# Retention attention and channel mixer on one core: batch 1's q loaded row per partition and turned by whole products, with a redone order

## The chip, the cores and the metric

One core of a Trainium2 chip runs the whole program in one launch. The metric is the device time of that launch in microseconds (us). Three runs of the kernel before gave 185.78, 186.19 and 189.02 us; their median is 186.19 us.

## The reference

```python
def _attn_ref(q, k, v):                    # q, k, v: (4, 8, 768, 64)
    gamma = 1.0 - 2.0 ** (-5.0 - np.arange(H))
    scale = 1.0 / np.sqrt(D)
    for t in range(S):
        state = gamma * state + np.einsum('bhd,bhe->bhde', k[:, :, t], v[:, :, t])
        y[:, :, t] = scale * np.einsum('bhd,bhde->bhe', q[:, :, t], state)
    ...
def _moe_ref(x, w_tok1, w_tok2, w_ch1, w_ch2):   # x: (4, 768, 512), the heads side by side
    h = np.maximum(x.transpose(0, 2, 1) @ w_tok1, 0.0) @ w_tok2
    u = x + h.transpose(0, 2, 1)
    h2 = np.maximum(u @ w_ch1, 0.0) @ w_ch2
    return u + h2
```

A decaying sum over time (one decay per head) gives y. The mixer then multiplies across time (768 to 256 to 768), adds, multiplies across channels (512 to 1536 to 512), and adds again. All inputs are float32; the kernel computes in float16 with float32 sums.

## The kernel before

**Tiling.** There are four batches of eight heads, and the heads go in pairs, so that a pair fills 128 columns (2 heads of 64). The 768 steps are cut into 6 chunks of 128. `front(b, p)` does the attention of pair p of batch b and the mixing over time; `back(b)` does the mixing over channels of a whole batch. The recurrence is computed by chunks: inside a chunk as masked scores (`L642`, then `L653` with the mask, then `L673`), between chunks through a 64x64 state per head (`L591` sums it per chunk, `L603` carries it on, `L621` and `L623` round it, `L699` applies it).

**The back.** For batch 0, `L829` does the first channel product directly. For the others `widen7` (`L898`) and for all of them `narrow7` (`L1051` and `L1061`) compute it with seven block products in place of eight. The sums and differences of weights that these need are made once, on VectorE: `L1156` (`wsum`) and `L1169`. Evacuations from PSUM are split over ScalarE and VectorE (`L845`, `L909`, `L918`, `L1068` and others).

**How q and k get their layout.** The scores need q and k with the head dimension on the partitions and time along the row. k arrives with one time step per partition (`L495`, 96 rows of packets in the planner's unit, float32 to float16 on the way), is multiplied by its decay in SBUF, one instruction per head (`decayed`, `L533` on ScalarE or `L535` on VectorE), and is turned in one of two ways given by the table `TURNS`, whose three letters are for k, q and u: "t" means six whole 128x128 products with the identity (`L561`) and one copy out of PSUM (`L574`); "x" means a transposing DMA from the SP queue (`L549`). q has a third way, "w": it arrives with six successive time steps per partition (`L492`, long rows), is turned unscaled by twelve half-array products, 64 columns each (`L559`), and is multiplied on the way out of PSUM by a table of decays that depends on time, `gq` in the tile `late` (`L569`, on VectorE). The tile `late` is later used again for the weight sums of `L1169`. Batches 0 and 1 have q in way "w", batches 2 and 3 in way "x".

**The order.** Nothing is scheduled at run time. Each piece of work is an `Op` with its ways (an engine and a cost). The string `ORDERED` gives the order of all ops, two characters per op (a number in base 62 in the order in which the program makes the ops), and `WAYS` has one digit per op that selects its engine where there are two. Filtered by engine, `ORDERED` is the queue of that engine, and each engine works through its queue in that order: PE (the matmuls), ACT, DVE, POOL (the loads, through one software DMA queue) and SP (stores and transposing DMAs). `arrange` (lines 111 to 253) walks through these queues with a table of costs to choose banks and buffers. Where PE has nothing to do in the first 21 us of that plan, products with zeros are put in (`L1196`).

**Loads.** POOL's queue starts with batch 0's q, k and v, then `wt` (the time weights, first and second part), then batch 1's, mixed with the channel weights `wc` (first `wc1`, whose four parts are a0 to a3, then `wc2`, parts b0 to b2), then batches 2 and 3.

Of the kernel before, what the change touches and what calls it, by code (L numbers as in the profile page):

```python
# [110 lines left out]
def arrange(ops, BANKS, seq, ways):  # L111
# [144 lines left out]

DIGITS = "0123456789abcdefghijklmnopqrstuvwxyzABCDEFGHIJKLMNOPQRSTUVWXYZ"
ORDERED = (
    "0e0c070d01080f05000h0306090g0i1h1i1l0m0a1j0j1k0b1m1V0n1W1v1w0k1R1x1S1y1A1T0l1z1n1U1B1o0o2r2s25261p2t1q0p292u"
    "1r2v2a1s1C0q311t322w0r1u3528331D361E1F0t1X1Y27342G1Z2K0s1G2F202x21222J2b232y2I240x1H2H2d2z2c1I0u2e2A2L2f2B2C"  # L260
    "3f2g1J0w2D3h1M1K2h2E3i1N0v372i1L2N2M382O2P392j0y1O3a2m3b2Q3g3c4L3j3d2R0D3k3e2k3l3m2S3n0A3o2n2T3p2l1P3q2W0z2U"
    "1Q3r2X2V2p0B4M3s2Z2o3t2Y3w0C303u5k3B4d3x3C3F2q490H3z4a3v3D3A4b4ead4cag3GaeaN0EaO3Eb23yaPavaf5lb30Faw3Paxah3Q"
    "aQ0Gaias3Tb4aR3SaZaSb03R0N4nb13H4p4f3Iap4qay3Jaq3Kaj4rar0Iaz4g3L3Vat3MaA4o3UaKau0R3NaLaB4h4iakaC3Oam4j4Han4k"
    "3WaE1dao3X0JaFalaH3Y02aIaD1fbhaMbk3ZaT1eaGaUaJ400MaV1gbb41be4Ibnbibc4lbp4204bo4Jbdbl430O4Kbfbm4519bjbr440Kb8"
    "461ab54mb6bsb9bg0Q1baWbaaX474s1cbPb70LaY4u4NbQ4VbJ4Obw4P4Xby4Ybx4Q4t5h5gbAbL0T5S4Rbtbz4w4S0S4v5P4ZbCbubB4xbU"
    "4W0U4Tbq4y4Ubv516q50bF0P4z5Q524A546n4DbD4B53bV5mbE555VbY4CbG4Ec5565n4F6r5T5W5i6sbK57bN5j5o5X585p5YbO48c95q59"
    "5Z5rbSbZ5s60c65Uca5u5tbMcebT5w615R5b5vcfbW5x625zc85BbXci6o5c5y6p7tc1c05D5Acj5CbR0W6t4Gc75Ecn6Y6uc25F0X6v5d6Z"
    "5a6w70cgco5G6x176V6y63ch6z5H640V5e5I655K5fcb66675J686ackcc5L6W6ccd695M6bcl5N0Y6d6Bcm5O6e6D0Z6E716fcr12cvcscM"
    "cw6g6FcNcxcA6hcycRcBcOctcS6jcucD6icUcP6kcC726CcE6m6HcTcV73cFd36lcK7u6AcH6XcWd1cL74dScId2cYcX7vdUd4cZ6G816J75"
    "117zdT7w6I7xd87A766KdX7BdVd910dZd5dY7Cczdb6Ld6e0dcdacGdWe16Mdd82e7e26Ndf84cQdi85e87De486dgdjdk7E6O77e579dl6P"  # L270
    "7y78dB7bdpdC6R7adqdm83d7dG7cds7ddHdrcpdtcJ7edndJ6Qc3dDd0dKdudI6S7ge37fdL7h7idz6U14dEdw7jdQdvdAdxdN16dR7kdedM"
    "6TdFdOe6eX15dh7lev8z7HeYdo877L7p88dPex7mdyez7K7n7IeG7F897o8Aef8aeA8Bew8CeB8beg7qeEeRcq7r7JeV7seF8cey8d8feC7G"
    "eIbH8jeWeH7M7OeJ7N8i7P7QeK13eT7ReZeN8e8g18f297eS9aeO7Sf398e9f07T8h8D8l8neL7UeD8E7Xeb7V8F9df1eU7YekeM7W80f68G"
    "ea7Z9eeled9Fec998k9f8meef48Hf78o9gc4ei9G9hbI8Ieo9if5eh9bf8f9ej9c8p8Jemepfa8q8Ken9HfdeP8Neq8r9j8Q8s8Oer8t8R8L"
    "8v8Pfh8ufyfefi9lesfzfm8w9nfDfn9mfAfEg6fffp8xfBfGfqfo9p8MfjfrfwfHfFfgfx8TfNfk8VfI8SfO8U9L9o8WfK9IfP8XfLft9Mfs"
    "fRfufQ8Y9kfCfSfUg7g89NfV8Z9r9tgb9J9O909Kg9gc9qfX9P91ge9QfY9sfW8ygfgd9ufZg49293ggg5g1fJgl9vg0gnflgmgig2949wgh"
    "gjgo96gE959xgsgagF9T9RfT9ygt9WgJ9z9X9BgKgLg39Ugvgu9VgwgM9SgGgNgpgx9AgCgHgTfv9YgOa0gU9Za1gya2gzgPgqgQgDhJa3hD"
    "gkhHgA9ChFa49EhIhOhEa5gRgIhMfMhPhKa6hNhhhSgBhGhQgrhLhlgShRhja9hmhVhTa7hihnaahWhUach1gVgZh2hYhqgXh0gWfchshrh4"
    "htgYh6h5hkethuhoabh3a8h8hphvh7hwh99DhahxhdhyhzhbhBhZeQhci3iki0i4iSilimi2i8i1i5i9ipheiri6iqibhAiaicinishCiZid"
    "fbitiieuhfifiuijiBigiwiIiCixiziDiTiGiEiUiHiXi7iVj9iYiJieiWjgiviAiKj0jsiLj1kRiQiFiNj2iRj7iOj4j8jbioj5jajqkBhg"  # L280
    "j6jejcjrktjfiPjvj3kCjhjwkujtjijyjxjjjzjojukJjkjljAjpjFjdkKjBjCjmjGk7iMihjDkvk3jEjLiyk4kwjnk5kxk8jHkLkcjMjJke"
    "jIkykfjSjQjTkdkijRkzkgkjkAk6jUkhjWjKjVkkk9jXklkDkEkakFhXjYkMkGjNkbk1kHkNkmkOjZjOkIkPjPknkQk0kqkokSk2kTkUkrkV"
    "kWkpkskXkY"
)
WAYS = (
    "000000000000000000000000000000000000000000000000000000000000000000000000000000001000000000010000000000000000"
    "100000100000001000000000000000000010110100101000000000000000000000000000010000000000000000000000000000000000"
    "110010011010001000011000000000000000000000100000000000000000000000000000000100100010000000000000000000000000"
    "001000000100000000000000000000000000000001001000000000000000000000000001100100000000000000000000000100000110"
    "010010000000000000000000000000001011001000000000000000000000000000001100100000000000000000000000000010000010"  # L290
    "000000000000000000000000000000001000000000000000010100000000101100100000100000000000000000000000000000000000"
    "000000000000000000000000000000000000000000000000000000000000001000000000000001000000000000000000000100000000"
    "000000000000011000000000000000000000000010000000000000000000000000000000001000000000100000000000000001000000"
    "000000000010000000000000000000000000000000000000000000001000000000000000000001000000000000000010000000000000"
    "000000100000000100001000000000100000000010000000000000000100010010000000000000000000000000000000010000000000"
    "000000000001100000100000000100000110000000000000000000000000000000000010100001000000100000000000000001000000"
    "000000000010010000000010000000100000001000000000000001100000000001000100010001000000000000000000000000000000"
    "00001"
)


# [1 line left out]
def kernel(  # L303
# [75 lines left out]
    def one(eng, cost, emit):  # L379
        return [(eng, cost[0], cost[1], emit)]  # L380
# [123 lines left out]
    def front(b, p):  # L504
# [14 lines left out]
        KT, QT = Slot("kT"), Slot("qT")  # L519
# [4 lines left out]
        def rows_of(j):  # L524
            return slice(j * D, (j + 1) * D)
# [19 lines left out]
        def turn(src, dst, dep, mode):  # L545
            if mode == "x":
                def emit():
                    t = tile_of(dst, [P, S], F16)
                    nc.sync.dma_start_transpose(out=t.rearrange("d (c t) -> d c t", t=P),  # L549
                                                in_=src.tile.rearrange("p c h d -> p (c h d)"))  # L550
                return Op(ops, (PLACE[b, p], 0, b, p, 0), [("SP", 1200, 1200, emit)], dep, [dst], [src], dma=(48, 28))
            T = Slot(FA)

            def emit():
                tp = tile_of(T, [P, 1024], F16)
                for c in range(NC):
                    if mode == "w":
                        for j in range(2):
                            nc.tensor.transpose(tp[rows_of(j), c * P:(c + 1) * P], src.tile[:, j, c], ident16)  # L559
                    else:  # L560
                        nc.tensor.transpose(tp[:, c * P:(c + 1) * P], src.tile[:, c].rearrange("p h d -> p (h d)"),  # L561
                                            ident16)
            t = op(one("PE", (350, 520) if mode == "w" else (336, 499), emit), dep + [ident_op], [T], [src], tiled="turn" if mode == "w" else "")
            if mode == "w":
                def emit():
                    d = tile_of(dst, [P, S], F16).rearrange("d (f p c) -> d f p c", f=2, c=NC)
                    o = T.tile[:, :S].rearrange("d (c f p) -> d f p c", f=2, c=NC)
                    w = LATE.tile[:, p:p + 1].rearrange("d o (p c) -> d o p c", c=NC).to_broadcast([P, 2, SH // NC, NC])
                    nc.vector.tensor_tensor(d, o, w, ALU.mult)  # L569
                return op(one("DVE", (870, 950), emit), [t, gq_op], [dst], [T, LATE])  # L570

            def emit(e):
                d, o = tile_of(dst, [P, S], F16), T.tile[:, :S]
                (nc.scalar.copy if e == "ACT" else nc.vector.tensor_copy)(d, o)  # L574
# [654 lines left out]
```

## Time and profile before

| | |
|---|---|
| median of three runs | 186.19 us |
| the profiled execution, its own time | 185.28 us |
| its span, first to last instruction | 183.5 us |
| PE (matmul) busy | 177.1 us, 97% |
| DVE (VectorE) busy | 168.9 us, 92% |
| ACT (ScalarE) busy | 137.5 us, 75% |
| POOL (GpSimd) busy | 53.8 us, 29% |
| DMA queue q0 (POOL's loads) | 67728 packets, 13.18 MB |
| granted TensorE clock | full speed throughout |

The profiled execution lies 0.9 us below the median of the runs, and 1.8 us of it lie outside the span. Matmuls are pipelined and each is recorded with its whole passage, so a busy PE is read better from the distance between successive starts: the chain of work that ended last gives that directly, since its pieces are cut at each start. In that chain a piece has its start, its length, its engine, the tile written and the line. In the groups by line, "x8 | 7.5, 944" means eight instructions, 7.5 us busy, 944 ns each. Vector instructions that follow each other overlap by some 80 ns, so sums of their lengths overstate a little.

### The profile page before, as it was taken

The numbers are of one execution on the slowest core, as the hardware profiler recorded it, in microseconds if no ns is written. First come the engines' busy times: TensorE is split into PE (matmuls) and PEld (weight loads), VectorE is DVE, ScalarE is ACT, GpSimd is POOL, SyncE is SP. The second block draws the span as 40 slices with busy tenths as digits, with TensorE's granted clock in tenths as the row PEclk, the third lists the DMA queues.
The fourth block names the chain that finished last, engine by engine and source line by source line (L and its number), as shares of the span: only waits on it lengthen the run. The fifth ranks groups of instructions, "written<-read, shape, count | busy, mean of one in ns | idle before, by whom it ended". The sixth has DMA issues, their size and how long they took to land.

```text
span 183.5 us, 5308 instructions
## 1 busy us (share of the span) xinstructions
PE 177.1 (97%) x2089; PEld 133.9 (73%) x2089; DVE 168.9 (92%) x450; ACT 137.5 (75%) x320; POOL 53.8 (29%) x63
## 2 busy tenths in 40 slices
PE   7789999999999999999999999999999999999993
PEld 3455898566789988866668899767778986566893
DVE  5699999989999899999999999998999989889893
ACT  6667899547979998899999896899975455688100
POOL 8997586553508008604051220000000000000000
PEclk9999999999999999999999999999999999999999
DMA  6999999999999999999999799702602333610046
GB/s 121 153 173 182 179 187 201 178 193 206 168 155 160 154 162 152 160 153 131 132 211 121 200 118 187 176 0 42 90 2 46 88 126 120 229 57 0 4 184 218
DMA packets 94137, 25.31 MB, mean 138 GB/s; under 512 B 83616, under 2 KB 91296, under 8 KB 94112
## 3 DMA queue, kind: packets, MB, share of 16 engines
q0 software_dynamic: 67728, 13.18, 85.6%
q1 hardware_dynamic: 24656, 9.31, 23.9%
q10 hardware_dynamic: 1728, 2.49, 4.0%
q8 instruction: 16, 0.26, 0.5%
q14 instruction: 9, 0.07, 0.1%
HBM read 26.74 MB, written 6.29 MB: 180 GB/s over the span
## 4 chain that ended last, share of the span: by engine, by line
PE 86%; POOL 5%; DMA 5%; DVE 2%; issue 0%; POOLq 0%
PE bank L898 22%; PE bank L1051 16%; PE bank L1061 12%; PE bank L829 9%; PE bank L750 6%; PE bank L730 6%; DMA wt<-in_moe_w_tok_dram 5%; PE bank L642 3%; PE bank L977 3%; PE bank L673 3%; PE bank L699 2%; PE bank L591 2%; POOL v L495 2%; POOL k L495 2%; POOL q L492 2%; PE bank L795 1%
## 5 line engine op out<-in xcount | busy, mean ns | idle before, releaser
L653 DVE TENSOR_TENSOR am<-bank,mask 128x384 f16<-128x384 f32 x64 | 32.9, 546 | 0.8 <-PE bank L642 0.8
L918 DVE TENSOR_TENSOR h<-bank,us 128x384 f16<-128x384 f32 x54 | 29.2, 550 | 1.7 <-PE bank L898 1.2
L909 ACT COPY us<-bank 128x384 f32<-128x384 f32 x51 | 23.4, 482 | 7.6 <-PE bank L898 7.2
L495 POOL DMA_DIRECT2D v<-in_v_dram x16 | 16.5, 1035 | 39.8 <-PE bank L699 17.9
L898 PE MATMUL bank<-hs,late 128*128 128x384 f16 x108 | 22.4, 326 | 0.0
L1068 DVE TENSOR_TENSOR X<-X,bank 128x256 f32<-128x256 f32 (+1 forms) x45 | 17.9, 405 | 2.1 <-PE bank L1061 1.7
L1051 PEld LDWEIGHTS <-hs 128*128 128x128 f16 x192 | 17.9, 98 | 2.5
L1041 ACT COPY us<-bank 128x256 f32<-128x256 f32 x27 | 9.9, 369 | 13.0 <-PE bank L1051 11.2
L898 PEld LDWEIGHTS <-late 128*128 128x128 f16 x144 | 13.2, 98 | 7.9 <-DVE hs L868 0.7
L603 DVE SCALAR_TENSOR_TENSOR U<-U,gp,bank 128x64 f32<-128x64 f32 x64 | 16.8, 272 | 1.1 <-ACT U L601 0.5
L1051 PE MATMUL bank<-wsum,hs 128*128 128x256 f16 x132 | 17.6, 273 | 0.0
L829 PE MATMUL bank<-uT,wc 128*128 128x384 f16 x96 | 17.2, 326 | 0.0
L621 ACT ACTIVATE cross<-U,gp 64x320 f16<-64x320 f32 x28 | 15.6, 558 | 2.0 <-DVE U L603 1.7
L495 POOL DMA_DIRECT2D k<-in_k_dram x15 | 15.4, 1026 | 4.9 <-DVE kT L574 2.1
L898 PE MATMUL bank<-uT,wc 128*128 128x384 f16 x72 | 16.3, 326 | 0.0
L750 PE MATMUL bank<-h,wt 128*128 128x128 f16 x192 | 15.0, 219 | 0.0
L715 ACT CAST x<-bank 128x384 f16<-128x384 f32 x31 | 14.7, 490 | 0.4 <-PE bank L699 0.4
L845 ACT ACTIVATE h<-bank 128x384 f16<-128x384 f32 x24 | 10.9, 503 | 5.2 <-PE bank L829 5.1
L898 PEld LDWEIGHTS <-wc 128*128 128x128 f16 x108 | 10.0, 98 | 5.8 <-issue 0.2
L1061 PEld LDWEIGHTS <-h 128*128 128x128 f16 x132 | 12.4, 98 | 2.0 <-DVE h L925 0.6
L750 PEld LDWEIGHTS <-wt 128*128 128x128 f16 x192 | 12.3, 98 | 1.8
L715 ACT COPY X<-bank 128x384 f32<-128x384 f32 x28 | 13.5, 496 | 0.0
(96 smaller groups left out, 393.7 us busy)
## 6 DMA issues: line engine op xcount, KB each, us to landing
out_dram<-X SPq DMA_DIRECT2D x14, 256.0 KB, 2.4
q<-in_q_dram POOLq DMA_DIRECT2D x16, 192.0 KB, 5.9
v<-in_v_dram POOLq DMA_DIRECT2D x16, 192.0 KB, 6.5
k<-in_k_dram POOLq DMA_DIRECT2D x15, 192.0 KB, 6.5
wc<-in_moe_w_ch_dram POOLq DMA_DIRECT2D x5, 512.0 KB, 13.9
out_dram<-X ACTq DMA_DIRECT2D x8, 256.0 KB, 2.6
wc<-in_moe_w_ch_dram POOLq DMA_DIRECT2D x2, 256.0 KB, 9.4
us<-in_k_dram SPq DMA_DIRECT2D x1, 384.0 KB, 3.4
```

Source lines behind the costliest of these rows:

```text
L495: (nc.sync if hard else nc.gpsimd).dma_start(out=tile_of(s, [P, 2, NC, D], FP if hard else F16), in_=src.rearrange("h (c p) d -> p (h c) d ...
L603: nc.vector.scalar_tensor_tensor(out=u[:, c], in0=u[:, c - 1], scalar=gp[:, p:p + 1], in1=st, op0=ALU.mult, op1=ALU.add)
L653: nc.vector.tensor_tensor(am, SC[g].tile[:, :m * P].rearrange("p (i t) -> p i t", t=P), mask.to_broadcast([P, m, P]), ALU.mult)
L715: (nc.scalar.copy if e == "ACT" else nc.vector.tensor_copy)(tile(), t)
L750: nc.tensor.matmul(Y[j].tile[:, 2 * i * D:2 * (i + 1) * D], wt2[:, jt, t], H1.tile[:, jt], start=False, stop=(jt == NJ - 1), skip_group_ch ...
L829: nc.tensor.matmul(acc[:, :SH], wc1[:, ct, ft * P:(ft + 1) * P], UT.tile[:, ct, sh * SH:(sh + 1) * SH], start=(ct == 0), stop=(ct == NP - 1))
L898: nc.tensor.matmul(acc[:, :SH], left(ct), r[:, ct], start=first and ct == 0, stop=ct == C2 - 1, skip_group_check=True)
L909: (nc.scalar.copy if e == "ACT" else nc.vector.tensor_copy)(ks[:, j], R1.tile[:, :SH])
L918: nc.vector.tensor_tensor(h(m, sh), R.tile[:, :SH], KS.tile[:, j], ALU.add)
L1051: nc.tensor.matmul(acc_[:, lo], l[:, j], r[:, j], start=first and j == 0, stop=j == K2 - 1, skip_group_check=True)
L1061: nc.tensor.matmul(acc_[:, lo], l[:, j], r[:, j], start=first and j == 0, stop=j == K2 - 1, skip_group_check=True)
L1068: (nc.vector if e == "DVE" else nc.gpsimd).tensor_tensor(dst(), dst(), b_(), ALU.add)
```

## The change

In the rows of `TURNS` for batch 1 the letter for q becomes "t" in place of "w". By this, for each of the four pairs of batch 1:

- q's load goes through `L495` in place of `L492`: one time step per partition, 1536 short rows in place of 256 long ones;
- two instructions scale it in SBUF by `gy`, one per head (`L533` or `L535`);
- six whole products turn it (`L561`) in place of twelve half-array ones (`L559`);
- a plain copy takes it out of PSUM, on ScalarE or VectorE (`L574`), in place of the multiplication by the table on VectorE (`L569`).

Batch 0 keeps way "w", so the table is still made. The number of ops grows by eight, from 1301 to 1309, and `ORDERED` and `WAYS` are new from end to end. The queues that they give differ in many places that have nothing to do with q: for example, ScalarE's list has four stores fewer and SP's four more, and the order of the loads is another.

```diff
@@ -256,46 +256,46 @@
 ORDERED = (
-    "0e0c070d01080f05000h0306090g0i1h1i1l0m0a1j0j1k0b1m1V0n1W1v1w0k1R1x1S1y1A1T0l1z1n1U1B1o0o2r2s25261p2t1q0p292u"
...
+    "0e08070d010c05000h0309060f0m0g1h1i0n1l1j1m0i1k0a0k1w1R1v0b1S1A0j1z1V1x1T1W0l1U2v1y2w0o1B261n2a250r351o1p1q1r"
...
 WAYS = (
...
@@ -344,7 +344,7 @@
-    TURNS = "twt twt twt twt twx twx twt twt xxx xxx xxx xxx xxx xxx xxx xxx".split()
+    TURNS = "twt twt twt twt ttx ttx ttt ttt xxx xxx xxx xxx xxx xxx xxx xxx".split()
     TURN = {(b, p, x): TURNS[NP * b + p][i] for b in range(B) for p in range(NP) for i, x in enumerate("kqu")}
@@ -578,7 +578,7 @@
             qt = turn(QF, QT, [qd], "w")
         else:
             Q, ql = decayed("q16", QF, qd, gy, False)
-            qt = turn(Q, QT, ql, "x")
+            qt = turn(Q, QT, ql, TURN[b, p, "q"])
```

POOL's queue up to the last `wc` part, read from the two strings (q12 is q of batch 1, pair 2):

```
before: q00 q01 k01 v00 k02 q02 k03 q03 v01 v02 t1 t2a t2b v03 q12 k10 q11 q10 q13 k11 a0 a2 a1 v10 v11 a3 k12 b1 b2 b0
after:  q00 k01 q01 q02 v00 q03 k02 v01 k03 v02 t1 v03 t2b t2a k11 k10 q10 v10 v11 a0 a2 q11 a3 a1 q12 k12 k13 b0 b1 b2
```

On PE, the four q turns of batch 1 stood ahead of the first `L829`, one between the time products of batch 0 and three in a row. Now the turns of q10, q11 and q12 stand among the `L829` and that of q13 among the products of `narrow7` of batch 0. Two groups of `L591` (states of pairs 0 and 1 of batch 1) have moved ahead of the first `L829` instead.

More of the change, by code (lines that the diff above doesn't have):

```diff
@@ L264 @@
[L264 to L278, printed above, removed]
@@ new lines @@
+    "270q2r1s2s291t362t0p1C1u2u1D281E0v312F1X2I322G2H1Y1F330s1Z1G2x2034212y222z2c232J2b0u2A241H2B2K2d2e2C1I2D0z3f"
+    "2f373i2g2L3h380B2E1M392h3a3b0y2N2M3c2i2O1J3d2P3g2Q2j0D3k1K2m3e1L2R3j2k0x3l1N3n2S3m3o3p2n2W1O2T3q0C2p2l4b3r02"
+    "2U4c2o2X1P0A3s4d3B3C3t1Q2Y3w0t2q2Z3u4e3J3x4j303D3K3y0H3z3L4k04al3Aao3M3vamaV3EanapaW2VaqaY0JaXaZ3N4lbg4mb73F"
+    "3GaA0G4nb83O3Hb9bhaB4f4gbibd3IaCaG4o4hb00E3R4iaH3SaD4p3Pba0FaE4q3Vbe3U3QaSax3T0wbfaP1daIaTayaQ0I1eazb1aRb23W"
+    "aU3Ybbb34L0LaJ1fbc4raFar4M4P4sas4Q4N4v3Xat3Z4tau0Q405maK4O414R4uaLaM4SaN421gaOav0M4351awbs535nbtbvbjbk52bmbl"
@@ new lines @@
+    "54bn5o550Sb4bw5p4w4y4x19444A0Nb5bobz1abu454zbp0K1b4BbqbA47br4C1cb60O4T4D5ubx4UbE46bR0W5v4E4V5qbG4W4FbSbFbB5w"
+    "4GbT5r4H6vbI5x4X5X4Y5sbC5YbVbH5y4ZbDbX4IbU50bK5zbY486wc2by4J4a497B5759c3bJ635tbL5658645ZbN0P65bWbM5ac6bO5b6y"
+    "ch60c761665c67cd5A62c0685dbZcice5Cc16x5B5e5Dcm5f5E69c45F4Kcn6z5H6a5G5Jcqcfc56A5L5Icg5Kcr5h0T5Mc97Ccv0R5ica5g"
+    "5j5Ncw0Uc86b5O6B6c125P6f5S5Qco6d6C0Z5T6D5k6e6g5Vcp5l0V6i6E6h5W6j6kcs6F14cz6lcj5R6GcA6H6m0Xck5UctcD6ncUcucE6J"
+    "73clcIcB6rcV6o6McJcZ746LcL76d0cW756Nd16pcXd2cM79cCd3cK7D776qcSd47ad96scNcFcT78d66KdacP8cd5dbd7e06tcQ6Pdc6Odd"
@@ new lines @@
+    "cG6I0Ydg7be2e17ccY6Qdh6R7d108d7H6Se3e57I6Tdj7e8918e7e67Jd8didk7Ke8de8adq17dle96Ue47f7Leadn6Vefdmdrdoecegds7M"
+    "7Eed6W7hebdt7FcH6XdJ7G7jdxdK7i6ZdydL7ldO708b7kdAdP7mdMdu7gdRdB8edz71dv7odSdQdC7n7q6u7pdTdH8H11dE8I7rdYeedUdI"
+    "dV9fbQ16dp6Y7sdDcOdfdWf5dZ15dF7teDdX8f7PdNf67udwcR7R7x7vdGeH7S8g7weEeJ7yeFeIen7A8KeK8h7zeM7Q7Neo8J8n7T7OeO8o"
+    "eNbP8i7V7U8j7WeQeP137Y8p7XeGeSeR7Z8keLel8leT8L80eZ8m8r8Mf3eU819geV8qf47282f09i85eh83f8f1868tei8v87889lf78Nf9"
+    "faeWem9m8O84epcc8s8ufbeqcx8P9nfeejer8Q9jes9o8R9N9p9kfffc8wf2eu8xet8Sfd9hekew9O9qevfgfhcycbexezfl8T8yfieAfpfm"
@@ L299 @@
+    "000010000000001000000000001000010001001000000000100000010000001001000000100000000000000000000000000100000010"
+    "000000000100000000001000000000000001000000100000000000000010000000000000000000001000000000000001010100000000"
+    "010000000001000010100100000000000000000000000000000100000000011000000000010000000110010010000000100000001000"
+    "0000100000000"
 )
```

40 lines of the change are left out of this document (18 added, 22 removed).

## The prediction

> **What bounds the kernel now.** I read the chain of work that ended last first, by engine on the page and then piece by piece, because the shares of busy time alone don't say which engine sets the end.
>
> ```profile
> PE 86%; POOL 5%; DMA 5%; DVE 2%; issue 0%; POOLq 0%
> 10.69 8.28 DMA wt<-in_moe_w_tok_dram
> 19.01 0.84 PE bank L730 x12
> ...
> 27.00 0.67 PE bank L730 x12
> ...
> 180.53 0.29 DVE X L986
> ```
>
> The reader is to see three stretches. Up to 18.97 us (10.69 + 8.28) the chain is loads: the time weights land, and only then can the first `L730` run. From 19.01 to about 180.5 it is PE. Then a last addition and a store make 3.0 us up to the span's end of 183.5. PE's pieces are 86% of 183.5, or 157.8 us, out of 161.5 us between 19.0 and 180.5, so only 3.7 us in that stretch are not matmuls. They are not many small holes of PE either. The longest place where the chain leaves PE is the handover from `widen7` to `narrow7` in batch 1, where the last h tiles are made:
>
> ```profile
> 93.15 1.00 DVE h L918 x2
> ...
> 95.94 0.61 PE bank L1061 x4
> ```
>
> Four pieces on DVE fill these 2.79 us, and even there PE mostly had other products to do. The table of 20 us windows shows it, and it also shows how near DVE and ACT are (columns: length, then PE, PEld, DVE, ACT, POOL busy and counts, clock, DMA share, GB/s):
>
> ```profile
> 20.00:40.00 20.00, 20.00 (x325) 15.49 (x322) 18.82 (x44) 16.00 (x35) 13.01 (x16) 1.00 1.73 186
> 40.00:60.00 20.00, 20.00 (x229) 15.69 (x227) 19.52 (x44) 16.84 (x42) 9.64 (x10) 1.00 2.02 174
> 60.00:80.00 20.00, 19.98 (x295) 16.82 (x292) 18.99 (x52) 18.50 (x47) 7.07 (x7) 1.00 1.80 157
> 80.00:100.00 20.00, 19.72 (x218) 13.74 (x217) 19.84 (x58) 19.07 (x50) 5.14 (x5) 1.00 1.40 156
> 100.00:120.00 20.00, 19.95 (x257) 16.68 (x255) 20.00 (x54) 16.85 (x42) 2.02 (x2) 1.00 0.97 157
> ```
>
> PE lacks 0.28 us in 80 to 100 and almost nothing elsewhere. DVE has 1.65 us free in the 80 us from 40 to 120 (80 less 19.52, 18.99, 19.84 and 20.00). ACT has 4.00 and 3.16 us free in the first two rows. So the kernel is bound by PE with DVE close behind. A change gains by what it takes from PE, by an earlier 19.0 us, or out of the 3.7 us; it loses wherever its order lets PE stand.
>
> **PE's part.** The four q turns of batch 1 stand in two places of the chain, and the products that k already uses stand later:
>
> ```profile
> 24.05 0.46 PE bank L559 x12
> 24.51 0.78 PE bank L730 x12
> ...
> 29.01 1.13 PE bank L559 x36
> 30.14 0.44 PE bank L795 x6
> ...
> 31.35 3.22 PE bank L829 x19
> ...
> 37.34 0.43 PE bank L591 x20
> ...
> 47.64 0.34 PE bank L561 x6
> ```
>
> Removed: 0.46 + 1.13 = 1.59 us. Added: four times six products at 0.34, which is 1.36. That is 0.23 us less. A half-array group also slows what follows it: `L730` took 0.78 at 24.51 where the one at 27.00 took 0.67, and the `L795` at 30.14 took 0.44 where the products of `L561`, of the same shape, took 0.34. Those two exits, 0.11 + 0.10, go too, since whole products don't change the array's shape. PE gains 0.44 us.
>
> **DVE's and ACT's part.** Per instruction, from the groups by line and form:
>
> ```profile
> L569 DVE TENSOR_TENSOR qT<-bank,late 128x768 f16<-128x768 f16 x8 | 7.5, 944 | 1.5 <-ACT k L533 0.9 <-PE bank L559 0.6
> L574 ACT COPY kT<-bank 128x768 f16<-128x768 f16 x6 | 4.8, 799 | 1.8 <-PE bank L561 1.8
> L574 DVE COPY kT<-bank 128x768 f16<-128x768 f16 x2 | 1.1, 547 | 0.3 <-PE bank L561 0.3
> L533 ACT ACTIVATE q<-q,gy 128x384 f16<-128x384 f16 x7 | 4.3, 613 | 0.0
> L535 DVE TENSOR_SCALAR q<-q,gy 128x384 f16<-128x384 f16 x9 | 2.6, 320 | 0.0
> L801 ACT COPY uT<-bank 128x768 f16<-128x768 f16 x4 | 3.3, 813 | 0.0
> L801 DVE COPY uT<-bank 128x768 f16<-128x768 f16 x2 | 1.1, 550 | 0.2 <-PE bank L795 0.2
> ```
>
> Counting ops by engine in the old and the new order gives how they fall. On DVE four `L569` go (3.78 us). Four copies at `L574` come, two of them k's that were ACT's before (2.19), and two scalings of q (0.64), and three copies of u move over from ACT (1.65). That is +0.7 us. On ACT six scalings of q come (3.68), two copies of q replace two of k, and the three copies of u go (2.44): +1.2 us. The remaining swaps between the two engines concern single evacuations; each engine gains and loses a few, and I allow +1 us for each. So DVE rises by 0.7 to 1.7 us against 1.65 us free in 40 to 120, and ACT by 1.2 to 2.2 against 7.2 free in 20 to 60, which is where most of q's work now stands. I cost both at nothing on the path. What hides them is the PE stream itself. If that cover fails on DVE, the price is up to the 1.7 us.
>
> **The loads' part.** What a short-row load takes in POOL's queue, against a long-row one, is read from when neighbours land. Start from the timeline of POOL, time to landing from the DMA issues of windows with just that one issue:
>
> ```profile
> 16.27 0.70 POOL L492 DMA_DIRECT2D q<-in_q_dram  x1 [0.54 <-PE bank L591]
> q<-in_q_dram POOLq DMA_DIRECT2D x1, 192.0 KB, 9.3
> 17.48 0.71 POOL L492 DMA_DIRECT2D q<-in_q_dram  x1 [0.51 <-PE bank L642]
> q<-in_q_dram POOLq DMA_DIRECT2D x1, 192.0 KB, 8.9
> 19.50 0.70 POOL L492 DMA_DIRECT2D q<-in_q_dram  x1 [1.32 <-DMA wt<-in_moe_w_tok_dram]
> q<-in_q_dram POOLq DMA_DIRECT2D x1, 192.0 KB, 7.9
> 20.91 1.04 POOL L495 DMA_DIRECT2D k<-in_k_dram  x1 [0.71 <-ACT x L715]
> k<-in_k_dram POOLq DMA_DIRECT2D x1, 192.0 KB, 7.7
> ...
> 32.80 0.74 POOL L475 DMA_DIRECT2D wc<-in_moe_w_ch_dram  x1 [1.79 <-DMA wc<-in_moe_w_ch_dram]
> wc<-in_moe_w_ch_dram POOLq DMA_DIRECT2D x1, 512.0 KB, 15.1
> ```
>
> They land at 25.57, 26.38, 27.40 and 28.61. A long-row load takes 0.81 and 1.02 us, mean 0.92; the short-row one behind them takes 1.21. The four loads lengthen the queue by 4 x 0.29, about 1.2 us. POOL's own issue grows from 0.70 to 1.04 each, which the landings 8 to 9 us later hide.
>
> At three places of the queue this can reach PE. First, the ten loads ahead of t1 are the same ten, so 19.0 us stays. But v03 now goes ahead of both t2 parts, which land 1.2 us later, while `L750` needs them soon after t1's products. Its cost lies between 0 (the attention products that the new order puts in between fill the time) and 1.2 us; I take the middle, 0.6. Second, the first `L829` needs a0, the first of these three issues:
>
> ```profile
> 21.95 2.25 POOL L475 DMA_DIRECT2D wc<-in_moe_w_ch_dram  x3
> wc<-in_moe_w_ch_dram POOLq DMA_DIRECT2D x1, 256.0 KB, 8.0
> ```
>
> It landed at 29.95. Ahead of it four long and two short loads (6.1 us) become five short ones (6.05) behind t2, so it lands when it did. PE arrives earlier than its old 31.35, by 1.59 + 0.21, and later by the two `L591` groups moved ahead (0.43) and the 0.6, hence at 30.6. I take 0, with 0.6 as the upper end if the queue runs another 1.2 us late. Third, the last part of `wc2` landed at 47.9 (32.80 + 15.1). Now three longer q loads and k13 stand ahead of it and q13 no longer does: +0.87 + 1.21 - 0.92, hence 49.1. The weight sums and the first product that uses them stand here:
>
> ```profile
> 48.49 0.95 DVE L1156 TENSOR_TENSOR wsum<-wc 128x1536 f16<-128x1536 f16 x1
> ...
> 51.55 0.95 DVE L1156 TENSOR_TENSOR wsum<-wc,wsum 128x1536 f16<-128x1536 f16 x1
> ```
>
> The four sums can begin at 49.1 in place of 48.49 and end 0.6 us later, at 53.1. The first product with `wsum` began at about 53.2 before and begins no earlier now, so I take 0, with 0.6 as the upper end.
>
> The Trainium skill speaks against the short rows. Its page "DMA: Bandwidth & Descriptors", section Specifications, puts the least transfer for full rate at 512 B and says that smaller ones cost a read-modify-write. The new load writes 128 B pieces. Were a short load to take twice a long one by this, the four would cost 3.7 us and not 1.2. The landings above, 1.21 against 0.92 for the same bytes, agree that short rows are slower and disagree with a factor of two.
>
> **The sum.** -0.23 - 0.21 + 0.6 = +0.16 us on the execution's own 185.28, or 185.44. The median of the runs is 0.91 above that execution, which makes 186.4 us: no change. From the bounds alone: below, -0.44 and perhaps the 0.28 us of idle PE in 80 to 100, 185.5; above, 0.44 less gained against t2 1.2, a0 0.6, `wsum` 0.6 and DVE 1.7, 189.9.
>
> **The rivals.**
>
> *DVE at the handovers (slower).* The order is new everywhere, and PE's stream before has almost no holes, so it has more to lose than to win. The place is where `widen7` ends and `narrow7` begins: PE needs the last h tiles from DVE. In the rows at 93.15 this took 2.79 us, of which all but 0.28 was covered by other products. If half of it is bare in the new order at the three handovers of batches 1 to 3, that costs 3 x 1.4 = 4.2 us, 190.6 us; if all, 194.5. It decides for a verdict of slower once about 1.3 us are bare at each. For it: DVE is full from 80 to 120 and receives more. Against it: at equal points of PE's queue, the amounts of DVE work queued ahead in the old and the new order differ by little.
>
> *Weights late (slightly slower).* Short rows take longer than 1.21 when they come in a row, as five do ahead of a0. With 1.8 each a0 would be 3.0 us late, of which PE's arrival at 30.6 leaves 2.3 bare: 188.7 us. It decides a loss from 0.7 us late on. Against it: k11, between other loads, took 1.21 in a queue that was full.
>
> *The holes close (faster).* If the new order left PE nothing to wait for after 19.0, the span would be 19.0 + 157.8 - 0.44 + 3.0 = 179.4, 4.1 us less, 182.1 us. For it: q's work leaves the crowded stretch before 31 us and goes where ACT had room. Against it: nearly all of the 3.7 us must go at once, and the change touches one batch's q.
>
> *The turn changes nothing by itself.* All four edits may be hidden, with the time decided by the order alone; that is the forecast's own time or one of the others, and has no chance of its own.
>
> **How the numbers follow.** No change 0.44, weights late 0.14, DVE at the handovers 0.36, holes closed 0.06. A measurement of this kernel can tell about 2% (3.7 us) from no change. The first two lie within it: same 0.58, slower 0.36, faster 0.06. The likeliest case's own range is 185.5 to 189.9. The range that should hold 8 of 10 goes a little way to the closed holes and over most of the bare handovers: 184.2 to 192.0.
>
> **What would show it.** Right: chain of PE from 19.0 on, with `L561` at 0.34 for q and no 0.78 behind it; `L750` starting by 21.4; the first `L829` at 30 to 31; `wsum` begun near 49; DVE's total up by 0.7 to 1.7 us. Wrong: DVE or ACT pieces of over 1 us in the chain at the start of a `narrow7`, PE below 19.5 in a 20 us window, or a wait of `L829` on `wc`. A first `L730` far from 19.0 would break the sum's first step.

## The result, and the profile after

The changed kernel took 187.44 us (median of six runs, 187.25 to 188.19), the kernel before beside it 186.14 us. The ratio is 1.0086, 95% interval 1.006 to 1.0111: slower by some 1.3 to 1.6 us, and within the 2% that the prediction called no change. The profiled execution of the changed kernel was its slowest, 188.19 us (span 186.4), 0.75 us above the median, so its losses read somewhat too large.

The chain of work that ended last, after the change (start, length, piece; first its shares by engine):

```profile
PE 74%; DMA 12%; POOL 6%; ACT 3%; DVE 2%; issue 1%; POOLq 0%; DVEq 0%
10.53 9.66 DMA wt<-in_moe_w_tok_dram
...
22.69 11.90 DMA wc<-in_moe_w_ch_dram
34.64 1.48 PE bank L829 x8
36.12 0.33 PE bank L561 x6
36.45 1.30 PE bank L829 x8
...
86.46 0.54 DVE h L918
...
88.96 0.83 PE bank L730 x12
...
96.00 0.62 ACT k L533
...
96.98 0.39 ACT h L952
...
98.16 0.39 ACT h L952
98.58 0.83 PE bank L1061 x6
...
182.91 0.29 DVE X L986
```

The time weights now land at 20.19 us (10.53 + 9.66) in place of 18.97. A second load has come into the chain: a2, part of `wc`, holds PE until 34.64. The q turns stand there as six whole products at 0.33, with nothing slowed behind them. At the handover of batch 1 the chain leaves PE twice, from 86 to 89 us for DVE's h and from 92 to 98.6 us for ACT's. The last addition starts 2.38 us later than before (182.91 against 180.53). From its end to the span's end there are 3.2 us, where it was 2.7.

The same in windows of 20 us, and what PE waited for (total, times, longest):

```profile
20.00:40.00 20.00, 19.36 (x284) 15.10 (x281) 17.77 (x49) 15.17 (x39) 11.28 (x13) 1.00 1.89 179
40.00:60.00 20.00, 20.00 (x245) 15.33 (x244) 19.32 (x42) 16.84 (x41) 9.14 (x10) 1.00 1.98 176
60.00:80.00 20.00, 20.00 (x290) 17.41 (x289) 18.78 (x51) 18.43 (x45) 9.09 (x9) 1.00 1.72 145
80.00:100.00 20.00, 18.62 (x206) 12.34 (x204) 19.96 (x56) 18.84 (x48) 7.59 (x7) 1.00 1.47 136
100.00:120.00 20.00, 20.00 (x264) 17.46 (x259) 19.96 (x56) 16.29 (x41) 1.01 (x1) 1.00 1.29 182
```

```profile
PE bank L1061 <- ACT h L952: 0.8, 1, 0.8
PE bank L730 <- DVE h L918: 0.4, 1, 0.4
PE bank L829 <- DMA wc<-in_moe_w_ch_dram: 0.3, 1, 0.3
```

PE is full from 40 to 80 us and from 100 to 120. It lacks 0.64 us between 20 and 40, where before it lacked nothing: some 0.3 ahead of its first `L730` and 0.35 in the wait for a2. It lacks 1.38 between 80 and 100, where before it lacked 0.28. So the losses to explain stand in three places: before 40 us, at the handover of batch 1 (1.1 us more than before), and at the last store (0.5 us). The steps that the prediction named are read from the timeline after:

```profile
20.27 0.83 PE L730 MATMUL bank<-x,wt 128*128 128x128 f16 x12
...
22.45 0.51 PE L750 MATMUL bank<-h,wt 128*128 128x128 f16 x6
...
51.42 0.95 DVE L1156 TENSOR_TENSOR wsum<-wc 128x1536 f16<-128x1536 f16 x1
...
183.33 0.33 SPq L992 DMA_DIRECT2D out_dram<-X  x1
```

### The profile page after: what moved, and what is told of

Same layout as the page of the kernel before. It is cut to its first block, busy times and chain, and to the rows that moved or that the text cites. A ratio compares the mean times of both kernels' runs of the same rounds, so it can differ in the third digit from the quotient of the medians.

```text
span 186.4 us, 5255 instructions
## 1 busy us (share of the span) xinstructions
PE 177.2 (95%) x2066; PEld 134.2 (72%) x2066; DVE 171.8 (92%) x454; ACT 137.2 (74%) x324; POOL 55.3 (30%) x63
## 4 chain that ended last, share of the span: by engine, by line
PE 74%; DMA 12%; POOL 6%; ACT 3%; DVE 2%; issue 1%; POOLq 0%; DVEq 0%
PE bank L898 19%; PE bank L1051 15%; PE bank L1061 12%; PE bank L829 7%; DMA wc<-in_moe_w_ch_dram 6%; DMA wt<-in_moe_w_tok_dram 5%; PE bank L750 4%; PE bank L730 4%; PE bank L642 3%; PE bank L977 3%; POOL v L495 2%; PE bank L673 2%; POOL k L495 2%; POOL q L492 2%; PE bank L699 1%
## 5 line engine op out<-in xcount | busy, mean ns | idle before, releaser
L918 DVE TENSOR_TENSOR h<-bank,us 128x384 f16<-128x384 f32 x54 | 28.2, 548 | 0.7 <-PE bank L898 0.4
L909 ACT COPY us<-bank 128x384 f32<-128x384 f32 x49 | 22.8, 487 | 7.1 <-PE bank L898 4.9
L495 POOL DMA_DIRECT2D v<-in_v_dram x16 | 16.8, 1052 | 37.3 <-PE bank L699 26.3
L1041 ACT COPY us<-bank 128x256 f32<-128x256 f32 x28 | 10.4, 382 | 13.4 <-PE bank L1051 13.2
L829 PE MATMUL bank<-uT,wc 128*128 128x384 f16 x96 | 17.8, 326 | 0.3 <-DMA wc<-in_moe_w_ch_dram 0.3
L495 POOL DMA_DIRECT2D k<-in_k_dram x15 | 15.5, 1031 | 4.2 <-DVE kT L574 1.5
L898 PE MATMUL bank<-uT,wc 128*128 128x384 f16 x72 | 16.4, 326 | 0.0
L621 ACT ACTIVATE cross<-U,gp 64x320 f16<-64x320 f32 x27 | 15.0, 558 | 0.9 <-issue 0.4
L750 PE MATMUL bank<-h,wt 128*128 128x128 f16 x192 | 14.7, 219 | 0.1
L715 ACT CAST u<-bank 128x384 f16<-128x384 f32 x27 | 13.1, 492 | 1.6 <-PE bank L750 1.5
L730 PE MATMUL bank<-x,wt 128*128 128x128 f16 x192 | 13.3, 219 | 0.6 <-DVE h L918 0.4
```

What stands on the lines that cost most here:

```text
L495: (nc.sync if hard else nc.gpsimd).dma_start(out=tile_of(s, [P, 2, NC, D], FP if hard else F16), in_=src.rearrange("h (c p) d -> p (h c) d ...
L715: (nc.scalar.copy if e == "ACT" else nc.vector.tensor_copy)(tile(), t)
L730: nc.tensor.matmul(acc[:, jt * P:(jt + 1) * P], wt1[:, i, jt * P:(jt + 1) * P], X16.tile[:, i].rearrange("p h d -> p (h d)"), start=(i == ...
L750: nc.tensor.matmul(Y[j].tile[:, 2 * i * D:2 * (i + 1) * D], wt2[:, jt, t], H1.tile[:, jt], start=False, stop=(jt == NJ - 1), skip_group_ch ...
L829: nc.tensor.matmul(acc[:, :SH], wc1[:, ct, ft * P:(ft + 1) * P], UT.tile[:, ct, sh * SH:(sh + 1) * SH], start=(ct == 0), stop=(ct == NP - 1))
L898: nc.tensor.matmul(acc[:, :SH], left(ct), r[:, ct], start=first and ct == 0, stop=ct == C2 - 1, skip_group_check=True)
```

## The experiments

Kernels run together share their runs of the kernel before (186.0 to 186.5 us), so results are compared by their ratio to it; 0.005 is 0.9 us.

**The load alone.** The kernel before, with only the load of batch 1's q changed to short rows. Its time steps then come out in another order.

```diff
-        wide = what == "q" and TURN[b, p, "q"] == "w"
+        wide = what == "q" and b == 0
```

> The kernel before with q of batch 1 loaded one row per partition and then treated as before, so that its time steps come out in another order: the load's part of the change alone, without scalings, turns or a new order. Theory A: the four loads lengthen the queue by 4 x 0.29 us, the last part of wc2 lands at about 49.1 in place of 47.9, the a0 part at 31.1 in place of 29.95, PE waits for it for at most 0.3 us, and the time is 186.1 to 186.5. Rival B: at least 1 us slower, 187.2 or more. [...]

Measured: 187.53 us, ratio 1.0063 (1.0031 to 1.0096): some 1.2 us slower, more than theory A allowed. PE's window, its wait and the load that it waits for:

```profile
20.00:40.00 20.00, 19.39 (x327) 15.42 (x325) 17.98 (x43) 16.06 (x35) 13.03 (x15) 1.00 1.99 176
```

```profile
PE bank L829 <- DMA wc<-in_moe_w_ch_dram: 0.6, 1, 0.6
```

```profile
22.95 11.95 DMA wc<-in_moe_w_ch_dram
...
34.94 1.47 PE bank L829 x8
```

The price of the rows is as the prediction had it. Behind t1 (19.46 here, 18.97 before) a0 landed 12.13 us later (31.59) where it took 10.98 (29.95). That is 1.15 us more for four loads, 0.29 each. But PE does not wait for a0. It waits for a2, which landed 3.30 us behind a0 in place of 2.57, though no load of q stands between the two. PE was ready for it at 34.33 us, so neither the 1.15 us nor the extra 0.73 us would have made it wait alone; together they make the 0.61 us that a full window now lacks. The rest of the 1.2 us is not placed: PE's first `L730` came at 20.19 us, 1.18 later, behind loads that this experiment leaves alone.

**The load undone under the new order.** The changed kernel with long rows for batch 1's q (again another order of its time steps). Per head a partition then holds one run of 768 B as written, in place of six of 128 B:

```diff
-        wide = what == "q" and TURN[b, p, "q"] == "w"
+        wide = what == "q" and b < 2
```

> The changed kernel with batch 1's q loaded in long rows again (768 B on a partition in place of three rows of 256 B), so its time steps come out in another order; scaling, turns and order as in the change. Theory L (four loads that take some 0.3 us more of the queue each make the expert weights late, and PE waits for them): a0 and a2 land 0.6 to 1.2 us earlier than with the change, PE's wait of 0.5 us for wc near 34 us goes, and the time is 186.3 to 186.9 us. Rival H (the bare handover of batch 1 sets the cost): 187.3 to 187.6 us, with PE's busy time between 80 and 100 us at 18.6 still.

Measured: ratio 1.0053 (1.0016 to 1.009). PE in the two windows:

```profile
20.00:40.00 20.00, 19.83 (x294) 15.72 (x294) 18.21 (x51) 15.96 (x40) 11.70 (x15) 1.00 1.73 185
...
80.00:100.00 20.00, 18.62 (x210) 12.41 (x209) 19.96 (x56) 18.82 (x47) 7.57 (x7) 1.00 1.44 137
```

The wait for `wc` is gone, a0 landed at 30.76 us and not 31.38, and the first window gets 0.47 us back. The handover does not move at all, so it does not hang on this load. Theory L seems to have the wait and the window on its side. But short rows alone do not bring the wait. The kernel of the next experiment has them, in the same order, and its window is as full:

```profile
20.00:40.00 20.00, 19.90 (x295) 15.29 (x294) 18.19 (x49) 15.43 (x39) 12.29 (x14) 1.00 1.89 179
```

Of the nine kernels here that have the change's short rows and its order between 30 and 40 us, only the change itself shows a wait for `wc`; the other eight lack 0.10 us or less in that stretch. So the wait belongs to one execution, in which a2 was late, and only the earlier landing of a0 can be put to the load. In time this kernel stands 0.6 us under the change, which their intervals do not separate. Theory L is not shown.

**The turns alone.** The changed kernel with batch 1's q turned by twelve half-array products, with all else as in the change:

```diff
+                    elif mode == "h":
+                        for j in range(2):
+                            nc.tensor.transpose(tp[rows_of(j), c * P:(c + 1) * P], src.tile[:, c, j], ident16)
...
-            qt = turn(Q, QT, ql, TURN[b, p, "q"])
+            qt = turn(Q, QT, ql, "h" if b == 1 else TURN[b, p, "q"])
```

> The changed kernel with batch 1's q, loaded and scaled as the change has it, turned by twelve half-array products again in place of six whole ones; copies, loads and order as in the change. By the prediction's term for PE (turns 0.23 us shorter, two exits from half-array mode 0.21): 187.8 to 188.0 us, about 0.4 to 0.5 above the changed kernel, with pieces of 0.40 to 0.46 for the turns in the chain and slower products behind them. Rival (PE's time at these places is hidden by waits for loads): 187.3 to 187.5 us.

Measured: 188.85 us, ratio 1.0124 (1.0081 to 1.0166). Three lines were put in, so `L829` is `L832` here. In its chain:

```profile
35.04 0.46 PE bank L562 x12
35.50 1.41 PE bank L832 x8
```

The same two pieces took 0.33 and 1.30 with whole products (36.12 and 36.45 above). So a turn gains 0.13 us, and the product behind it 0.11, as the prediction had it from other lines. In time this kernel stands 0.7 us above the change. The intervals overlap, so a gain of the forecast's 0.44 us fits, and so does none.

**The change in the old order.** The kernel before with the change's table, load, scaling (all on VectorE) and whole turns, the turns put just ahead of the first `L829`:

```diff
-    TURNS = "twt twt twt twt twx twx twt twt xxx xxx xxx xxx xxx xxx xxx xxx".split()
+    TURNS = "twt twt twt twt ttx ttx ttt ttt xxx xxx xxx xxx xxx xxx xxx xxx".split()
...
-            qt = turn(Q, QT, ql, "x")
+            qt = turn(Q, QT, ql, TURN[b, p, "q"])
```

> The kernel before with the whole change of batch 1's q (short rows, two scalings each, six whole products, plain copy) but with the old order kept: only the eight scalings are put in, on VectorE, the four turns stand together just ahead of the first channel products, and the small op that makes gy is moved ahead of them. Theory A: PE saves 0.44 us, VectorE is even (four times 0.47 us less for the copy, eight scalings of 0.23 more), the weights land 1.2 us later; the time is 185.6 to 186.6, so the change itself costs nothing and the loss is that of the new order. Rival B: 187.2 or more, with PE waiting before the first channel products.

Measured: 191.43 us, ratio 1.027 (1.0229 to 1.0311). Its windows, the first of 20 us and two shorter ones inside it, and its longest wait:

```profile
20.00:40.00 20.00, 16.91 (x241) 13.85 (x240) 15.29 (x42) 13.07 (x29) 13.35 (x15) 0.91 1.99 175
...
28.00:32.00 4.00, 2.52 (x42) 2.12 (x38) 3.04 (x11) 3.15 (x8) 2.71 (x5) 1.00 1.59 194
32.00:34.00 2.00, 0.90 (x11) 0.79 (x9) 2.00 (x7) 0.00 (x0) 0.73 (x1) 0.67 1.41 197
```

```profile
PE bank L561 <- DVE q L535: 3.0, 4, 1.1
```

Theory A, that the change costs nothing in the old order, falls; PE waits ahead of the first `L829`, as B has it. A turn of scaled q waits for its scaling, which a turn of unscaled q did not: 3.0 us at four turns. Part of that is this placing: VectorE itself stood 0.96 us for `gy` ahead of the first scaling. The new order has none of these waits. It puts the turns among the `L829`, 0.5 to 1.1 us behind the end of their scaling, and is 3.4 us or so faster than this placing (1.027 to 1.0086).

**The start.** Three kernels tried the order of the first loads. First the changed kernel with only the eleven first loads as before, then the kernel before with those of the change:

```diff
 POOL's queue in the changed kernel, up to t1
-q00 k01 q01 q02 v00 q03 k02 v01 k03 v02 t1
+q00 q01 k01 v00 k02 q02 k03 q03 v01 v02 t1
```

> The changed kernel with one thing put back: the first eleven loads of POOL's queue in the order of the kernel before (q00 q01 k01 v00 k02 q02 k03 q03 v01 v02 t1). Theory A, that the order of these loads made t1 land 1.2 us later and that PE's dense stretch starts with t1: t1 lands near 19.0, the first time product starts at 19.0 to 19.2, and the time falls by 1.0 to 1.3 us, to about 186.3. Rival B, that the loss comes from the turn of q itself (short rows, scalings, copies): t1 may land earlier, but PE waits for the channel weights or on the handover instead, and the time stays within 0.4 us of 187.4.

> The kernel before with one thing changed: the first eleven loads of POOL's queue in the order of the changed kernel (q00 k01 q01 q02 v00 q03 k02 v01 k03 v02 t1). Theory A: t1 lands at 20.0 to 20.3, and the time rises by 1.0 to 1.3 us, to about 187.3. Rival B: the same bytes in another order cost nothing, 186.1 within 0.4 us.

Measured: 188.65 us, ratio 1.0121 (1.0087 to 1.0155), and 188.34 us, ratio 1.0086 (1.0054 to 1.0119). The times of theory A and of rival B were missed in both. The first `L730` of either:

```profile
20.99 0.83 PE L730 MATMUL bank<-x,wt 128*128 128x128 f16 x12
```

```profile
22.43 0.83 PE L730 MATMUL bank<-x,wt 128*128 128x128 f16 x12
```

In the first, t1 landed at 19.29 us and PE still began at 20.99, since its own queue now waits for q and k in the other order. In the second it waits even longer. The loads cannot be judged without the queues that use them. So a third kernel took all engines' order up to about 17 us, and the loads up to v03, from before:

```diff
 ORDERED, WAYS of the changed kernel
-    first 138 places: as in the change
+    first 138 places: as before, without the loads of batch 1
```

> The changed kernel whose order starts as before: all engines' work up to about 17 us, and the loads up to v03, in the order of before; batch 1's q and everything later as in the change. In the profiles so far t1 landed at 18.97 to 19.58 us wherever the first loads stood in the old order and at 19.82 to 20.75 wherever they stood in the new one. Theory S (the start costs the change some 0.9 us, which stays to the end): t1 at 19.0 to 19.6, the first L829 at 30.3 to 30.9, time 186.3 to 186.7 us. Rival W (the wait of L829 for a0, a2 and b's parts of wc takes up what the start gives): first L829 at 31.3 to 31.6 still, time 187.2 to 187.6.

Measured: 188.19 us, ratio 1.013 (1.0087 to 1.0173). Its timeline and its longest wait between 20 and 40 us:

```profile
19.40 0.84 PE L730 MATMUL bank<-x,wt 128*128 128x128 f16 x12
...
31.69 4.06 PE L829 MATMUL bank<-uT,wc 128*128 128x384 f16 x24
```

```profile
PE bank L699 <- DVE cross L623: 0.7, 1, 0.7
```

The start came 0.87 us earlier, as theory S asked, and the first `L829` no earlier than in the change (31.53 there). So theory S falls. Rival W is nearer, though both its numbers were passed and its cause is not there: PE waits for VectorE, not for `wc`. Over all profiles t1 landed at 18.97 to 19.58 us in six kernels with the old first loads and at 19.82 to 20.75 in eight with the new ones. The same ten loads in another order cost 0.85 us in the mean; none of the runs shows that this reaches the end.

**The handover.** First eight pieces were moved by hand behind the h tiles they stood ahead of:

```diff
 queues at the handover of batch 1
-ACT: k L533, X L715 ahead of the last h L952
+ACT: both behind it
-DVE: two k and two q scalings L535, two adds L603 ahead of h tiles
+DVE: all six behind pieces that make h (L918, L925)
```

> The changed kernel with nothing moved but what stood ahead of batch 1's last h tiles at the handover to narrow7: on ACT the scaling of one k tile and the copy of one X tile go behind the last-but-one relu of L952; on DVE two scalings of k, two of q and two adds of L605 go behind additions of L926 and L919 that make h. Loads, scaling and turns of q stay as the change has them. Theory H (about 1.1 us of the change's cost is bare at this handover, because ACT and DVE have q's and k's pieces of batch 2 queued ahead of h): PE's busy time between 80 and 100 us goes from 18.62 back to about 19.7, and the time is 186.1 to 186.5 us, 1.0 to 1.3 below the changed kernel. Rival L (the cost arises early, by the longer row loads, and a smoother handover only passes it on to the next wait): 187.2 to 187.6 us, whatever PE does between 80 and 100.

Measured: 188.16 us, ratio 1.0097 (1.0069 to 1.0124): no gain. PE's window, its new wait and the piece of VectorE that stands ahead of it:

```profile
80.00:100.00 20.00, 18.83 (x210) 12.68 (x209) 19.74 (x56) 18.50 (x47) 7.53 (x7) 1.00 1.36 135
```

```profile
PE bank L898 <- DVE h L918: 1.2, 1, 1.2
```

```profile
88.28 0.91 DVE L535 TENSOR_SCALAR q<-q,gy 128x384 f16<-128x384 f16 x1
```

The hole moved to an earlier h. A scaling that was put off now stands there, stretched to 0.91 us. Eight pieces do not undo an order. So the whole order was taken back, from three points on:

```diff
 ORDERED, WAYS of the changed kernel, from about 52 us on (after q's last piece)
-    as in the change
+    as before
 DVE's queue ahead of narrow7 of batch 1
-  L918 L909 L918 x3 L535 (k) L925 x2 L535 (k) L925 x3
+  L918 L925 L918 L925 L918 x2 L925 L918 L925 x3
```

> The changed kernel whose order ends as before: from about 52 us on, after the last piece of batch 1's q, every engine's work, with its choice between VectorE and ScalarE, as before; start, loads and q as in the change. Theory O (of the change's cost, about 1.1 us is the handover of batch 1 and 0.5 us the last stores, both made by the redone order and neither by q): PE's busy time between 80 and 100 us 19.7, last store 2.6 us from issue to the end in place of 3.1, time 185.6 to 186.0 us. Rival Q (q's scaling and copies on VectorE and ScalarE leave these engines late by the handover, whatever the order): PE at 18.6 to 19.0 there, time 186.9 to 187.5.

With the old start as well:

> The changed kernel with both: start and rest in the order of before, only the stretch from about 17 to 52 us, in which batch 1's q is loaded, scaled and turned, as in the change. If theories S and O both hold and add: t1 at 19.0 to 19.6, PE at 19.7 between 80 and 100 us, time 184.8 to 185.4 us, about 0.5% under the kernel before, the gain being the 0.44 us of PE's turns and fewer waits before 50 us. If one of them falls: 185.7 to 186.6 us. If the loss is a cost of q itself that only changes its place: 187.2 to 187.6.

Measured: 194.26 us, ratio 1.0444 (1.0401 to 1.0487), and 194.87 us, ratio 1.0481 (1.0437 to 1.0524). Neither expectation was met. In the first:

```profile
PE bank L642 <- DVE X L1068: 4.5, 1, 4.5
```

This one wait ends at 78 us, behind a q that landed at 77.01. In the change's loads k and q of batch 2, pair 2, come last of that batch; the old order of PE asks for them first. A fault of the splice, not of q. The same with the loads of batches 2 and 3 as before:

```diff
 POOL's queue in the kernel above, behind v13
-k21 k20 k23 q20 v20 q21 v23 v21 v22 k22 q22 k30 ...
+q20 k22 k20 q21 v20 k21 v22 k23 q22 v21 v23 k30 ...
```

> As the run before last but one, the change up to about 52 us and the order of before from there, but with the loads of batches 2 and 3 in the order of before too, so that the k and q that PE needs at 72 us are no longer the last of batch 2. Theory O: no window of 20 us behind 60 us with PE under 19.6, last store 2.6 us, ratio 0.999 to 1.003. Rival Q: a hole of 0.8 us or more in PE at the handover, about 85 to 98 us, ratio 1.005 to 1.009. If loads of batch 2 are late because the longer queue begins them late: a wait of PE for q or k between 60 and 80 us, of 0.5 to 2 us.

Measured: 193.71 us, ratio 1.0421 (1.0376 to 1.0466). The hole only moved forward, to 62 us, behind a k that landed at 61.63, and was larger than the 0.5 to 2 us expected of late loads:

```profile
PE bank L1051 <- DVE U L603: 4.2, 1, 4.2
```

In the traces the engines' work first differs from the change's at 70 to 72 us in the kernels from 52 us on (a swap of equal pieces would not show), so 52 us is no point of the execution; in this kernel loads of before met an order that was still the change's. The last splice begins at about 82 us and leaves all loads alone; VectorE first differs at 87 us in its trace:

```diff
 ORDERED, WAYS of the changed kernel, PE, ACT, DVE and SP from about 82 us on
-    as in the change
+    as before
```

> The changed kernel with the order of before, and its choice between VectorE and ScalarE, from about 82 us on; all loads, and all work up to there, stay as in the change, so that nothing of batch 2 is asked for before it is loaded. Theory O (the handover of batch 1, 1.1 us, and the last stores, 0.5 us, are made by the redone order): PE's busy time between 80 and 100 us 19.5 to 19.8, last store 2.6 us from issue to the end, ratio to before 0.999 to 1.003 where the change has 1.0086. Rival Q (VectorE and ScalarE are late already at 82 us because of q's scaling and copies): PE 18.6 to 19.0 there, ratio 1.005 to 1.009. If the two orders don't fit where they are joined, a hole of PE of over 1 us stands right behind 82 us.

Measured: 187.01 us, ratio 1.0044 (1.002 to 1.0069).

```profile
80.00:100.00 20.00, 19.65 (x217) 12.90 (x216) 19.79 (x56) 19.30 (x49) 7.20 (x7) 1.00 1.59 140
```

```profile
183.02 0.33 SPq L992 DMA_DIRECT2D out_dram<-X  x1
```

PE has 1.03 us of its 1.10 back, and from this store's issue to the span's end (185.66 us) there are 2.64 us, as before (180.84 to 183.48), where the change has 3.10 (183.33 to 186.43). Both places are as theory O said, and both repeat. Five kernels with the change's order there (the change, the first loads put back, long rows, half-array turns, the old start) all have PE at 18.62 between 80 and 100 us. From the last store's issue to the span's end there are 2.98 to 3.13 us in the six profiles with the new end and 2.60 to 2.64 in the eight with the old one. Rival Q falls: up to 82 us VectorE and ScalarE had the change's queues, with all of q's scalings and copies in them. In time 0.8 us come back, half of what the two places add up to, and the ratio stays above the range that O gave; the intervals of this kernel and of the change overlap between 1.006 and 1.0069. No version tried is faster than the kernel before.

## Why the prediction was right, and where its steps were not

It was right that the change is too small to tell from none at 2%. The time, 187.44 us, came out 1.0 us above the forecast's 186.4, inside both ranges. That owes something to the width of the ranges: the forecast's +0.16 us is a gain that is in the rows and an allowance for t2 that was not needed, and the losses stand at places that the sum put at nothing. Point by point:

**PE's part** was right. The turns are 0.33 pieces in the chain, the slowed products behind them are gone, and with half-array turns put back both terms returned, 0.13 us on a turn that stands alone and 0.11 behind it. That the time falls by 0.44 us for it was not shown.

**DVE's and ACT's part** was right in the terms that it names. Counts times lengths from the groups give DVE +0.7 us for them and ACT some 2 us in all, as forecast; ACT's busy time is 0.3 us less all the same, since its instructions overlap more. DVE's total, though, rose by 2.9 us (168.9 to 171.8) against 0.7 to 1.7. Some 0.7 of it are two constants made once at the start, `ident` and `mask` (`L421`, `L447`), at 0.54 and 0.61 us in place of 0.23 each. The rest is the allowance for other swaps, which was too small. DVE's copies at `L909`, evacuations at the handovers, were three before; by the groups by line, in the change:

```profile
L909 DVE COPY us<-bank 128x384 f32<-128x384 f32 x5 | 2.7, 549 | 0.2 <-PE bank L898 0.2
```

and with the old order from 82 us on:

```profile
L909 DVE COPY us<-bank 128x384 f32<-128x384 f32 x3 | 1.7, 554 | 0.5 <-PE bank L898 0.5
```

There the two copies, 1.0 us, are off DVE again, and PE's time is back with them. That they alone hold PE up was not tried apart.

**The loads' part** failed at its first step, "19.0 us stays": the same ten loads in the new order let t1 land 1.2 us later in this profile and 0.85 in the mean. The first `L730` came at 20.27. The steps behind it held. The t2 parts landed at 22.41 and 23.38, 1.2 us later behind t1 than before, and `L750` followed at 22.45 and not by 21.4; but PE had other products and no hole from 20.27 to 30, so the allowance of 0.6 was not paid. From t1 to a0 there were 11.0 us before and 11.2 now. The sign listed as wrong, a wait of `L829` for `wc`, did appear, yet not for a0, which landed at 31.38 in place of 29.95: the 0.35 us were spent on a2, which the sum does not have, and no other kernel of this order shows such a wait. *Weights late* is not borne out: the five short loads ahead of a0 took 6.7 us, 1.34 each and not 1.8. The weight sums began at 51.42 and not near 49, because t1's shift and a2's came on top; PE is full there, so the 0 taken for them was right.

**The handover** is where the rival *DVE at the handovers* was right in kind. PE came to 18.62 in its window, under 19.5, and DVE and ACT pieces stand in the chain. The price was 1.1 us at batch 1 and nothing at the two later handovers (PE lacks 0.02 us from 100 to 180), under the 1.3 at each from which it decides. (Its 194.5 for three bare handovers should read 194.8 if it starts from the forecast, as its 190.6 does.) The forecast had put this place at nothing because the amounts of DVE work queued at equal points differ by little; no view here tests that count. The chain puts the last wait on ACT, with a scaling of k directly ahead of two h tiles. That such neighbours make the loss is likely but not shown, since moving eight of them by hand did not help; shown is that the order from 82 us on makes it.

**The end** was not in the sum at all: 0.5 us more for the last store. In the change two stores of `L992` follow each other as its last two; in the old order one does. What in the order of the stores lengthens it was not tried apart.

So the forecast's +0.16 us became 1.6 by the ratio. Some 0.8 of it came back with the old order from 82 us on (handover and last store). The rest, and the 0.44 that PE gains, would leave some 1.2 us without a place in the times, an estimate from ratios that are each uncertain by half a microsecond. The later first `L730` is the likeliest place, but a start as before did not make the kernel faster, so this stays open.

## What to carry to other kernels

When an operand is scaled before its turn instead of after it, the scaling becomes something the tensor engine waits for; a good order hides that. An order that is redone as a whole can bring costs of its own far from the edit (here at 85 to 98 us and at the last store, for an edit at 24 to 59 us), and they need not be the edit's: with the old order from 82 us on they went and the edit stayed. In a sum over a reordered program, take the landing of each load from its own place in the queue and carry every shift on to the next landing. When one profile shows a wait, look for it in the other profiles of the same order before putting it to the edit. At a handover, read the order of the pieces ahead of the awaited one, and not only how much work is queued there.

## What the runs showed of the hardware

**VectorE while GpSimd issues loads.** The changed kernel's timeline at the handover:

```profile
85.06 1.01 POOL L495 DMA_DIRECT2D v<-in_v_dram  x1 [7.15 <-PE bank L673]
...
85.34 0.79 DVE L925 TENSOR_SCALAR h<-h 128x384 f16<-128x384 f16 x1
...
90.12 0.24 DVE L925 TENSOR_SCALAR h<-h 128x384 f16<-128x384 f16 x1
```

The same instruction takes 0.79 us while a load is being issued and 0.24 when none is. It ends about when the issue does. Not every one is caught: of the seven `L925` on VectorE that began during an issue, three took 0.72 to 0.79 us and four 0.24; of the 26 others none took over 0.26. The Trainium skill, page "SBUF — State Buffer", section "SBUF: two separate sides", says that GpSimd and VectorE share one pair of ports, that an instruction of either that needs it locks it exclusively, and that the loser waits for the whole instruction; the stretched rows agree. The 0.91 us scaling in the experiment with eight moved pieces fits too: it began at 88.28, and a load was being issued from 88.05 to 89.11.

**The clock after a hole.** Windows of 4 us of the kernel with the old order from 52 us on, behind its 4.2 us hole (the column behind POOL's is the granted clock):

```profile
58.00:62.00 4.00, 0.48 (x8) 0.36 (x6) 0.35 (x2) 0.97 (x2) 0.00 (x0) 0.98 2.44 157
62.00:66.00 4.00, 3.28 (x16) 2.36 (x16) 3.00 (x11) 3.20 (x8) 0.00 (x0) 0.50 1.16 77
66.00:70.00 4.00, 4.00 (x45) 3.13 (x44) 2.48 (x8) 1.41 (x4) 0.47 (x1) 0.66 0.51 98
```

PE comes back at half its clock and has full clock for part of the third window only. So the hole is paid for again behind it, which fits that this splice and the first one stand 6.3 and 6.8 us above the change for single waits of 4.2 and 4.5. The Trainium skill, page "TensorE: Matmul & The Clock Gate", section "Part 1: The HAM clock gate", gives half rate after an idle window of about 3.4 us, and this trace agrees. One kernel differs: with the turn in the old order, no wait was longer than 1.1 us, yet between 28 and 34 us PE was busy for 3.42 of 6 us and its clock fell to 0.67 (rows in that experiment). So it takes no unbroken idle stretch of that length.

**Instruction fetches among the loads.** In the changed kernel a2 landed 3.21 us behind a0, where the same load took 2.53 to 2.57 in eight others. In the stretch from 31.3 to 32.5 us the DMA queues show, beside the loads:

```profile
q8 instruction: 1, 0.02, 5.1%
```

A fetch is not enough to delay a load. In the kernel with its first loads put back and in the one with long rows a fetch also began 0.5 us behind a0's landing, and a2 still took 2.54 us. What made a2 late stays open.
